# One addition on VectorE split by column: epsilon on the softmax sums of two heads

## The chip, the core and the metric

The kernel runs on one core of a Trainium2 chip. The metric is device time in microseconds (us) of one execution of the whole program. The names of the engines are those of the profile: PE is TensorE's matrix multiplication and PEld its weight load, DVE is VectorE, ACT is ScalarE, POOL is GpSimd, SP issues most transfers. Each engine works through its own instructions in the order in which they stand in the program, and waits where an instruction needs another engine's result.

## What is computed

Attention that keeps the 32 largest scores of each row, then a feed-forward layer, then a layer of 8 experts of which each token uses two.

```python
def _attn_ref(q, k, v):                       # batch 4, heads 8, sequence 576, head size 64
    scores = scale * np.matmul(q, k.transpose(0, 1, 3, 2))
    kth = np.partition(scores, -top_k, axis=-1)[..., -top_k:-top_k + 1]    # top_k = 32
    scores = np.where(scores >= kth, scores, -1000000000.0)
    scores = scores - np.max(scores, axis=-1, keepdims=True)
    attn = np.exp(scores)
    attn = attn / (np.sum(attn, axis=-1, keepdims=True) + 1e-09)
    return np.matmul(attn, v)
...
def _moe_ref(x, w_in, w_out):                 # 2304 tokens, 512 -> 2048 -> 512
    h = np.maximum(x @ w_in, 0.0)
    return h * h @ w_out
...
def _moe2_ref(x, ...):                        # the two best of 8 experts for each token
    out[mask] += top2_w[mask, k, None] * (np.maximum(x[mask] @ w1[e], 0.0) @ w2[e])
```

## The kernel before

Attention is cut into 80 units. A unit is 128 query rows of two heads (64 units, `pair_full`) or the 64 query rows left over, of two heads side by side on the partitions (16 units, `pair_left`). For each head of a unit PE makes 128 x 576 scores (L356), ACT copies them out of PSUM into `sb` (L359), and DVE searches the 32nd largest value: six pieces of 96 columns with MAX8 and MATCH_REPLACE8 (L367, L368), then rounds on the candidates (L369, L372, L374). POOL makes the bounds (`keep`, L390), ACT and POOL build the mask (L394, L395), and ACT takes the exponential and, in the same instruction, its sum over the row into one column of `sm` (L396). So in a full unit `sm` has two columns, one for each head; in a left unit one column is used.

`recip` then adds epsilon to `sm` (L401) and takes the reciprocal (L402), both on DVE. POOL spreads it (`rb`, L428), PE transposes the weights and `rb` (L407, L430, L431) and multiplies by V (L444), and DVE scales the result into `x` (L416, or L420 for left units). ACT and POOL split `x` into two parts for the matmuls of the next layer (L421, L422).

Units overlap: unit i + 2 is started while unit i is finished. Between these steps the program issues pieces of the feed-forward layer of tokens that are done (`step`; PE L272 to L288, ACT L292 to L295, POOL L296), of the routing, and, for the first 32 of 80 units, the conversion of the feed-forward weights (DVE L149 and L150, POOL L152 and L156). All of attention lies in the first 811 us. After it stand what is left of the feed-forward layer and the experts (PE L518 to L573).

A scheduler places the instructions: it keeps a priority for each (the order of the program, moved by an offset; `recip` and `finish` are moved ahead by 300, the feed-forward pieces back by 350) and a simulated time line, and so one instruction more can shift the order of others.

Of the kernel before, what the change touches and what calls it, by code (L numbers as in the profile page):

```python
# [14 lines left out]
ALU = mybir.AluOpType  # L15
# [4 lines left out]
EPS = 1e-9  # L20
# [32 lines left out]
def attention_ffn_moe(ctx: ExitStack, tc: tile.TileContext, q, k, v, w_ffn, w_route, noise, w_exp, out,  # L53
# [3 lines left out]
    nc = tc.nc  # L57
# [46 lines left out]
    for t, (b, i) in enumerate(tiles):  # L104
        if i == 0:
            nc.gpsimd.iota(tok_i[:, t:t + NFULL], pattern=[[P, NFULL]], base=b * S, channel_multiplier=1)
        elif i is None:
            nc.gpsimd.iota(tok_i[:, t:t + 1], pattern=[[0, 1]], base=b * S + NFULL * P, channel_multiplier=1)
            nc.gpsimd.tensor_scalar(tok_i[LEFT:P, t:t + 1], tok_i[LEFT:P, t:t + 1], 1.0, float(S - LEFT),
                                    op0=ALU.mult, op1=ALU.add)  # L110
# [287 lines left out]

    def recip(sm):
        with tc.high_priority(SOON):  # L400
            nc.vector.tensor_scalar(sm, sm, 1.0, EPS, op0=ALU.mult, op1=ALU.add)  # L401
            nc.vector.reciprocal(sm, sm)  # L402

    def transpose4(e):
# [43 lines left out]
    def pair_full(b, j, qt):  # L448

        hA = 2 * j  # L450
        q0 = 2 * (j % 2)
        es = []
        sm = apool.tile([P, 2], F32, name="sm", bufs=6)
        lf = apool.tile([P, 2, D], F32, name="lf", bufs=4)
        for i in range(2):
            kt = K4[b, j // 2][:, (hA + i) % 4]
            t = scores([(qt[:, 0, q0 + i, :], kt), (qt[:, 1, q0 + i, :], kt)])
            softmax(*t, sm[:, i:i + 1])
            left_keys(lf, i, t[0])
            es.append(t[0])  # L460
            yield
        recip(sm)
        pts = [transpose4(es[0])]
        yield
        pts.append(transpose4(es[1]))
        yield
        t5 = rest(es, sm, lf)
        yield
        yield times_v(b, hA, pts, t5)

    def pair_left(b, j, qt):
        hA = 2 * j
        q0 = 2 * (j % 2)
        st = []
        for i in range(2):
            kt = K4[b, j // 2][:, (hA + i) % 4]
            st += [(qt[:, 0, q0 + i, :], kt), (qt[:, 1, q0 + i, :], kt)]
        sm = apool.tile([P, 2], F32, name="sm", bufs=6)
        lf = apool.tile([P, 2, D], F32, name="lf", bufs=4)
        t = scores(st)  # L480
        e = t[0]
        softmax(*t, sm[:, 0:1])
        for i in range(2):
            left_keys(lf, i, e)
        yield
        yield
        recip(sm[:, 0:1])
        pt = transpose4(e)
        yield
        yield  # L490
        t5 = rest([e, e], sm[:, 0:1].to_broadcast([P, 2]), lf)
        yield
        yield times_v(b, hA, [pt, pt], t5)
# [302 lines left out]
    for e in range(E):  # L796
        nc.vector.tensor_scalar(over[:, e:e + 1], base[:, e:e + 1], float(-(e * NT + CAP)), 0.0,
                                op0=ALU.add, op1=ALU.max)
# [180 lines left out]
```

## Time and profile before

| | before |
|---|---|
| median of 3 runs | 1419.05 us (1416.67 to 1421.17) |
| the profiled execution | 1419.02 us |
| its span, first to last instruction | 1417.2 us |
| PE busy | 1261.8 us (89%) |
| DVE busy | 970.6 us (68%) |
| ACT busy | 844.6 us (60%) |
| POOL busy | 798.2 us (56%) |

The profiled execution lies 1.8 us above its span, and at the median. The shares are means over two very different stages: attention, up to about 811 us, and what follows. Matmuls overlap one another in the records, so a PE that is busy all the time is not thereby at its peak.

### The profile page before, as it was taken

The numbers are of one execution on the slowest core, as the hardware profiler recorded it, in microseconds if no ns is written. First come the engines' busy times: TensorE is split into PE (matmuls) and PEld (weight loads), VectorE is DVE, ScalarE is ACT, GpSimd is POOL, SyncE is SP. The second block draws the span as 40 slices with busy tenths as digits, with TensorE's granted clock in tenths as the row PEclk, the third lists the DMA queues.
The fourth block names the chain that finished last, engine by engine and source line by source line (L and its number), as shares of the span: only waits on it lengthen the run. The fifth ranks groups of instructions, "written<-read, shape, count | busy, mean of one in ns | idle before, by whom it ended". The sixth has DMA issues, their size and how long they took to land. (4 is left out here: it accounts for less than half of the span.)

```text
span 1417.2 us, 26382 instructions
## 1 busy us (share of the span) xinstructions
PE 1261.8 (89%) x7937; PEld 1085.0 (77%) x7937; DVE 970.6 (68%) x5025; ACT 844.6 (60%) x1741; POOL 798.2 (56%) x1366
## 2 busy tenths in 40 slices
PE   2576559899899899999999999999989999999996
PEld 1354347787788788787887888789778999989995
DVE  8999989999988899999999100145563434444342
ACT  5768768888886887897887534344443233333321
POOL 4869889896787776877756532605233315133131
PEclk9877769999999999999999999999999999999998
DMA  9984558961557345535533586836564435344241
GB/s 328 346 306 151 188 170 295 314 236 61 167 192 259 105 139 180 189 127 175 178 105 120 193 276 214 284 112 231 185 215 141 146 112 163 116 146 135 89 144 37
DMA packets 85241, 257.50 MB, mean 182 GB/s; under 512 B 10716, under 2 KB 10844, under 8 KB 85088
## 3 DMA queue, kind: packets, MB, share of 16 engines
q1 hardware_dynamic: 75808, 227.32, 48.5%
q0 software_dynamic: 9280, 28.40, 5.5%
q8 instruction: 65, 1.06, 0.3%
q14 instruction: 88, 0.72, 0.2%
HBM read 205.71 MB, written 52.06 MB: 182 GB/s over the span
## 5 line engine op out<-in xcount | busy, mean ns | idle before, releaser
L395 POOL TENSOR_TENSOR sb<-sb,w 128x576 f32<-128x576 f32 x144 | 207.6, 1448 | 17.8 <-ACT w L394 14.5
L368 DVE MATCH_REPLACE8 w<-m,sb 128x96 f32<-128x96 f32 x864 | 200.8, 242 | 0.0
L578 DVE SCALAR_TENSOR_TENSOR ht<-ph,ht 128x384 fp32r<-128x384 f32 (+1 forms) x128 | 62.7, 490 | 182.1 <-ACT ht L577 181.9
L577 ACT ACTIVATE ht<-ph 128x384 fp32r<-128x384 f32 (+1 forms) x128 | 55.9, 437 | 216.5 <-PE ph L573 216.5
L593 POOL DMA_INDIRECT out<-y,info x40 | 44.9, 1122 | 244.6 <-DVE y L592 238.0
L367 DVE MAX8 m<-sb 128x8 f32<-128x96 f32 x864 | 165.1, 244 | 19.3 <-ACT sb L359 16.1
L356 PE MATMUL ps<-K,qt 128*128 128x288 f32 x640 | 133.6, 335 | 40.1 <-POOL K L324 15.9
L571 PE MATMUL ph<-xe,wi 128*128 128x384 f32 (+1 forms) x512 | 159.6, 312 | 2.5 <-DVE xe L523 2.2
L572 PE MATMUL ph<-xe,wi 128*128 128x384 f32 (+1 forms) x512 | 159.5, 312 | 0.8 <-DVE xe L523 0.8
L573 PE MATMUL ph<-xe,wi 128*128 128x384 f32 (+1 forms) x512 | 159.2, 311 | 0.2 <-DVE wi L565 0.2
L356 PEld LDWEIGHTS ps<-K,qt 128*128 128x128 f32 x640 | 104.5, 210 | 52.6 <-ACT sb L359 20.1
L296 POOL TENSOR_TENSOR gt<-r,gt 128x384 fp32r<-128x384 f32 x96 | 97.8, 1019 | 63.6 <-ACT gt L295 57.7
L407 PE MATMUL pa<-ident,sb 128*128 128x128 f32 x576 | 99.4, 297 | 36.2 <-DVE x L416 13.0
L552 PE MATMUL acc<-wo,ht 128*128 128x512 f32 x320 | 126.5, 398 | 0.9 <-DVE y L592 0.8
L286 PE MATMUL pf<-xT,wi 128*128 128x384 f32 x320 | 115.4, 361 | 13.3 <-ACT r L292 5.8
L394 ACT ACTIVATE w<-sb,keep 128x576 f32<-128x576 f32 x144 | 110.2, 776 | 26.3 <-POOL keep L390 25.9
L553 PE MATMUL acc<-wo,ht 128*128 128x512 f32 x320 | 125.4, 394 | 0.0
L396 ACT ACTIVATE sb<-sb,keep 128x576 f32<-128x576 f32 x144 | 112.2, 780 | 21.2 <-POOL sb L395 20.9
L287 PE MATMUL pf<-xT,wi 128*128 128x384 f32 x320 | 111.9, 350 | 4.8 <-POOL xT L422 4.8
L272 PE MATMUL acc<-wo,gt 128*128 128x512 f32 x288 | 112.8, 403 | 3.0 <-DMA wo<-wsc 1.5
L407 PEld LDWEIGHTS pa<-ident,sb 128*128 128x128 f32 x576 | 68.2, 149 | 60.8 <-issue 22.8
L273 PE MATMUL acc<-wo,gt 128*128 128x512 f32 x288 | 111.0, 396 | 0.0
(181 smaller groups left out, 3547.8 us busy)
## 6 DMA issues: line engine op xcount, KB each, us to landing
wi<-wsc SPq DMA_DIRECT2D x96, 512.0 KB, 4.5
wo<-wsc SPq DMA_DIRECT2D x96, 512.0 KB, 4.5
raww<-in_exp SPq DMA_DIRECT2D x80, 512.0 KB, 3.6
raw<-in_ffn SPq DMA_DIRECT2D x32, 512.0 KB, 4.3
wsc<-csp SPq DMA_DIRECT2D x32, 512.0 KB, 3.9
xs<-xr SPq DMA_DIRECT2D x40, 258.0 KB, 7.4
mr<-xs SPq DMA_DIRECT2D x40, 258.0 KB, 3.4
qn<-in_q SPq DMA_DIRECT2D x40, 256.0 KB, 3.7
```

The source lines that it names most:

```text
L272: nc.tensor.matmul(acc[tt], gt[:, 0, sl], wo[:, 0, :], start=(f == 0), stop=False)
L286: nc.tensor.matmul(ph[:, 0:n], wi[:, 0, sl], xT[:, 0, c, 0:n], start=(c == 0), stop=False)
L356: nc.tensor.matmul(ps[:, n, 0:HS], st, kt[:, n * HS:(n + 1) * HS], start=(i == 0), stop=(i == len(pairs) - 1))
L367: nc.vector.max(top, sb[:, sl])
L368: nc.vector.match_replace(out=w[:, sl], in_to_replace=top, in_values=sb[:, sl], imm_value=NEG)
L395: nc.gpsimd.tensor_tensor(sb, sb, w, op=ALU.subtract)
L407: nc.tensor.transpose(pt[:, c * P:(c + 1) * P], e[:, c * P:(c + 1) * P], ident)
L552: nc.tensor.matmul(acc[t], hs[i][:, 0, sl], wo[:, 0, :], start=(f == 0), stop=False)
L553: nc.tensor.matmul(acc[t], hs[i][:, 0, sl], wo[:, 1, :], start=False, stop=False)
L571: nc.tensor.matmul(ph[:, 0:n], wi[:, 0, sl], xe[i][:, 0, c, :], start=(c == 0), stop=False)
L572: nc.tensor.matmul(ph[:, 0:n], wi[:, 0, sl], xe[i][:, 1, c, :], start=False, stop=False)
L573: nc.tensor.matmul(ph[:, 0:n], wi[:, 1, sl], xe[i][:, 0, c, :], start=False, stop=(c == NC - 1))
```

## The change

The addition of epsilon is issued once for each column of `sm`, where it was one instruction on all columns. The 64 full units have two columns, so they issue two additions in place of one. The 16 left units hand over one column and keep their one instruction. The reciprocal stays one instruction on all columns. Since a line is added, what stood at L402 and below is one line lower after the change (the additions at L402, the reciprocal at L403, and so on).

```diff
     def recip(sm):
         with tc.high_priority(SOON):
-            nc.vector.tensor_scalar(sm, sm, 1.0, EPS, op0=ALU.mult, op1=ALU.add)
+            for i in range(sm.shape[1]):
+                nc.vector.tensor_scalar(sm[:, i:i + 1], sm[:, i:i + 1], 1.0, EPS, op0=ALU.mult, op1=ALU.add)
             nc.vector.reciprocal(sm, sm)
```

DVE's rows of the second unit's start, while the first unit's two heads wait for their sums. Before the change, the search of one head stands there without an addition:

```order
L372 MAX m<-cand 128x8
L367 MAX m<-sb 128x8 x6
L368 MATCH_REPLACE w<-m,sb 128x96 x6
L367 MAX m<-sb 128x8
L369 MAX m<-w 128x8
L367 MAX m<-sb 128x8 x5
L372 MAX m<-m 128x8
```

After the change:

```order
L372 MAX m<-cand 128x8
L367 MAX m<-sb 128x8 x6
L368 MATCH_REPLACE w<-m,sb 128x96 x6
L402 TENSOR_SCALAR sm<-sm 128x1
L367 MAX m<-sb 128x8
L369 MAX m<-w 128x8
L367 MAX m<-sb 128x8 x5
L372 MAX m<-m 128x8
```

The addition for the unit's first head now stands here by itself, ahead of the pieces of the next head.

Some rows further on DVE, one search later, stands the addition that was there before, and the reciprocal. Before the change:

```order
L367 MAX m<-sb 128x8 x6
L368 MATCH_REPLACE w<-m,sb 128x96 x6
L401 TENSOR_SCALAR sm<-sm 128x2
L367 MAX m<-sb 128x8
L369 MAX m<-w 128x8
L402 RECIPROCAL sm<-sm 128x2
L368 MATCH_REPLACE w<-m,sb 128x96 x6
```

After the change:

```order
L367 MAX m<-sb 128x8 x6
L368 MATCH_REPLACE w<-m,sb 128x96 x6
L402 TENSOR_SCALAR sm<-sm 128x1
L367 MAX m<-sb 128x8
L369 MAX m<-w 128x8
L403 RECIPROCAL sm<-sm 128x2
L368 MATCH_REPLACE w<-m,sb 128x96 x6
```

The second head's addition keeps the place of the old one, on one column, and the reciprocal stays where it was. From the third unit on, the finer order of all engines differs at many places; DVE has 64 rows of attention more, no other engine has more or fewer.

## Rows read from the trace of the kernel before

**Rows 1.** Busy us (instructions) of each engine by stretch; granted clock, DMA share, GB/s.

```profile
core 0: us, PE busy (x) PEld busy (x) DVE busy (x) ACT busy (x) POOL busy (x), PEclk, DMA share, GB/s
50.00:100.00 50.00, 28.68 (x191) 21.89 (x192) 48.78 (x301) 33.98 (x67) 33.52 (x47) 0.73 0.98 350
100.00:200.00 100.00, 57.40 (x352) 43.17 (x353) 95.80 (x534) 76.45 (x153) 88.13 (x108) 0.69 0.49 168
200.00:300.00 100.00, 88.50 (x564) 75.89 (x561) 95.14 (x530) 82.86 (x172) 92.36 (x107) 0.94 0.82 278
300.00:400.00 100.00, 93.22 (x696) 77.30 (x696) 98.84 (x663) 85.44 (x186) 75.36 (x137) 1.00 0.43 139
400.00:500.00 100.00, 95.23 (x679) 80.88 (x677) 86.22 (x571) 74.27 (x161) 74.02 (x116) 0.97 0.54 184
500.00:600.00 100.00, 97.14 (x692) 83.55 (x692) 93.14 (x608) 83.30 (x178) 75.54 (x130) 1.00 0.51 173
600.00:700.00 100.00, 95.05 (x685) 82.48 (x684) 98.03 (x658) 82.38 (x179) 72.80 (x131) 0.98 0.49 158
700.00:780.00 80.00, 77.14 (x572) 63.68 (x571) 76.18 (x504) 63.01 (x138) 50.02 (x104) 1.00 0.36 120
780.00:813.00 33.00, 33.00 (x238) 28.32 (x238) 5.71 (x18) 17.30 (x40) 17.59 (x27) 1.00 0.56 186
...
1100.00:1300.00 200.00, 200.00 (x1138) 181.04 (x1137) 87.11 (x145) 62.79 (x125) 59.79 (x125) 1.00 0.43 135
```

**Rows 2.** PE in order of time near 305 us: start, us, instruction.

```profile
305.07 0.34 PE L287 MATMUL pf<-xT,wi 128*128 128x384 f32 x1
305.25 0.34 PE L288 MATMUL pf<-xT,wi 128*128 128x384 f32 x1
```

**Rows 3.** DVE groups by shape, whole span: busy us, mean ns, idle before.

```profile
L401 DVE TENSOR_SCALAR sm<-sm 128x2 f32<-128x2 f32 x64 | 36.8, 575 | 4.1 <-ACT sb L396 3.9
...
L401 DVE TENSOR_SCALAR sm<-sm 128x1 f32<-128x1 f32 x16 | 2.2, 139 | 1.3 <-ACT sb L396 1.3
```

**Rows 4.** Line L401 alone: duration ns min/median/max, first and last start.

```profile
L401 DVE TENSOR_SCALAR sm<-sm x80: 127/167/3485, 42.7 to 788.9; 128x2 f32<-128x2 f32 x64, 128x1 f32<-128x1 f32 x16
```

**Rows 5.** All engines in order of time, 300.2 to 301.4 us.

```profile
300.31 1.00 POOL L296 TENSOR_TENSOR gt<-r,gt 128x384 fp32r<-128x384 f32 x1
300.38 0.21 DVE L372 MAX8 m<-cand 128x8 f32<-128x56 f32 x1
...
300.50 0.84 DVE L401 TENSOR_SCALAR sm<-sm 128x2 f32<-128x2 f32 x1
...
301.25 0.28 DVE L416 TENSOR_TENSOR x<-pa,t 128x128 f32<-128x128 f32 x1
```

**Rows 6.** All engines in order of time, 113.4 to 113.8 us.

```profile
113.48 1.28 POOL L324 TENSOR_TENSOR qt<-qn,qt 128x512 fp32r<-128x512 f32 x1
113.54 0.14 DVE L401 TENSOR_SCALAR sm<-sm 128x1 f32<-128x1 f32 x1
...
113.59 0.08 DVE L368 MATCH_VALUE_LOAD w<-m,sb 128x8 f32 x1
```

**Rows 7.** DVE groups by shape, 0 to 300 us.

```profile
L401 DVE TENSOR_SCALAR sm<-sm 128x2 f32<-128x2 f32 x20 | 15.4, 771 | 0.0
...
L401 DVE TENSOR_SCALAR sm<-sm 128x1 f32<-128x1 f32 x4 | 0.5, 134 | 0.0
```

**Rows 8.** DVE's waits, 40 to 800 us: total us, times, longest.

```profile
DVE m L367 <- ACT sb L359: 15.7, 12, 3.6
DVE x L416 <- PE pa L444: 12.3, 5, 5.7
DVE sm L401 <- ACT sb L396: 5.2, 5, 1.4
```

**Rows 9.** PE's waits, 40 to 800 us.

```profile
PE pa L407 <- DVE x L416: 13.0, 7, 3.9
```

**Rows 10.** DVE in order of time at the end of attention.

```profile
780.24 1.57 DVE L785 TENSOR_TENSOR late<-keep 128x144 f32<-128x144 f32 x1 [0.42 <-POOL keep L390]
...
811.00 0.29 DVE L416 TENSOR_TENSOR x<-pa,t 128x128 f32<-128x128 f32 x1 [4.84 <-PE pa L444]
```

## The prediction

> **What bounds the kernel now.** I first read the busy time by stretch, because the shares on the page are means over two stages. Up to 780 us DVE is the fullest engine in most stretches: 48.78 of 50 us, then 95.80, 95.14 and 98.84 of 100 [rows 1]. PE, the engine with the largest total, is at 57.40 of 100 us between 100 and 200 us. Its 93 to 97 later on look like a full engine and are not: two matmuls of the feed-forward layer start 0.18 us apart where nothing holds them, and each is booked for 0.34 us [rows 2]. So PE has room during attention, and it waits for DVE there, for example 13.0 us at L407 for DVE's `x` [rows 9]. POOL comes near its end only between 200 and 300 us, with 92.36 of 100 [rows 1].
>
> After the last search the picture turns. DVE compares the kept bounds of all searches at 780.24 us, and its last `x` is at 811.00 us, after a wait for PE [rows 10]; PE is busy for all 33.00 us of that stretch, and for 200.00 of 200 us among the experts [rows 1]. So the time is, roughly, what DVE needs for its searches up to 780 us, plus a fixed piece of PE work behind it. Time that DVE saves before 780 us can shorten the whole; after it DVE's time is worth nothing, and the change touches nothing there, since the last addition starts at 788.9 us [rows 4].
>
> **What the changed instruction costs today.** The groups by shape hold the main finding. The addition on two columns takes 575 ns in the mean, 64 times, 36.8 us; on one column the same operation takes 139 ns, 16 times [rows 3]. One more column can't cost 436 ns of arithmetic. The line's durations run from 127 ns over a median of 167 to 3485 [rows 4], so most instances are short and a part of them is held for a long time while it is booked as busy. The order in time shows by what: at 300.50 us a two-column addition starts while POOL is in a TENSOR_TENSOR from 300.31 to 301.31, and it ends at 301.34, just behind POOL's end [rows 5]. A one-column addition at 113.54 us falls inside a POOL instruction of 1.28 us and still takes 0.14 us [rows 6]. None of the 16 can have been held long: with a minimum of 127 ns [rows 4] and a mean of 139 [rows 3], the longest is at most 16 x 139 - 15 x 127 = 319 ns.
>
> The Trainium skill has a rule for this: "SBUF — State Buffer", section "Who interferes with whom", says that VectorE in a mode that uses two ports and GpSimd exclude each other from a shared port pair for a whole instruction, and that tensor_scalar is an operation that can enter such a mode. The rows of the two-column form agree.
>
> **The sum.** Each full unit trades one two-column addition for two one-column ones.
> - Removed: 64 x 575 ns = 36.8 us. Added: 128 x 139 ns = 17.8 us. By durations DVE gains 19.0 us [rows 3].
> - DVE instructions overlap at their edges: the next one starts at 301.25, 0.09 us before the addition's end at 301.34 [rows 5], and at 113.59, 0.09 us before 113.68 [rows 6]. Each of the 64 additional instructions hides as much, 5.8 us in all, so by starts the gain is up to 24.8 us. I take the middle, 22 us, and keep 19.0 and 24.8 as bounds.
> - Where it falls: up to 300 us 20 of the 64 take 15.4 us; 40 short ones would take 40 x 0.139 = 5.6 [rows 7, 3], a gain of 9.8 of 19.0, or 52%. Of the 22 us, 11.4 lie before 300 us and 10.6 after.
> - What of it passes on: between 50 and 300 us DVE is busy for 239.7 of 250 us, but POOL is at 92.36 in the last 100 of them [rows 1] and would stop some of it; I let 80% pass, 9.1 us. From 300 to 780 us DVE is busy for 452.4 of 480 us, so it idles for 27.6 us [rows 1], mostly for scores from ACT and products from PE [rows 8]. Where DVE gets ahead of those it only waits longer; I let 60% pass, 6.4 us. Both shares are choices, the first nearer to all since almost no idle time stands there.
> - What is added besides: the first head's addition now stands alone in DVE's queue, ahead of the pieces of the next search, and waits for its own exponential. Behind it stand those searches, and behind them ACT, PE and POOL of the next heads. Today 5 of the 80 additions wait, for 5.2 us in all [rows 8]; 64 more at that rate would wait 4.2 us. A third of it falls on time that counts, the rest where DVE would have waited for scores anyway: 1.5 us. The bounds are nothing and the full 4.2.
> - The reciprocal, the DMAs and the instructions of PE, ACT and POOL stay the same in number. The scheduler's order moves them finely. Counted in the two orders, 1545 of the 2016 matmuls of the feed-forward layer stand ahead of attention's last product with V before the change and 1557 after it, so nearly the same work is left behind; I cost this at nothing. If PE had no room for those 12 during attention, they would be worth 12 x 0.18 = 2.2 us [rows 2] the other way.
>
> 9.1 + 6.4 - 1.5 = 14.0 us, against the profiled execution's 1419.02 us, which is the median's 1419.05 within 0.1: **1405.0 us**. The least by the bounds is 19.0 x 0.4 - 4.2 = 3.4 us gained (1415.6), the most all of 24.8 (1394).
>
> **The rivals.** 0.3%, or 4.3 us, is about what a measurement can tell from no change.
> - The gain is absorbed. DVE gets ahead and waits instead, for scores from ACT or products from PE, since ACT and PE are at 82 to 97 of 100 us after 200 us [rows 1], and for POOL between 200 and 300 us. With a quarter of 22 us passed on less 1.5, the time is 1415; with none, 1419 to 1420. For it speaks that a POOL that is held up less or more hides such shifts; against it that DVE idles for only 27.6 of 480 us [rows 1].
> - Slower: the first head's addition stops DVE's queue. It sits one search earlier than the joint one and needs the exponential of its head, which comes last in a chain of ACT and POOL. A wait today is 5.2 / 5 = 1.04 us [rows 8]. From a mean of 22 / 64 = 0.34 us for each of the 64 the gain is eaten; if every second waited for 1.04 us, DVE would lose 33 us against 22, and at 0.7 passed on the time would be 1419 + 8 = 1427. Against it: 75 of 80 additions wait for nothing today.
> - The change doesn't do what it says: the one-column form is held as well. Then 128 x 0.575 = 73.6 us stand in place of 36.8, and at 0.7 passed on the time would be 1419 + 26 = 1445. The 16 one-column rows speak against it [rows 3, 6]. The Trainium skill, "VectorE: DVE Perf Modes", section "What auto-detection actually checks", lets the two-port mode begin where the outermost dimensions other than one are even or equal in source and destination, and a single column in place is equal to itself; taken so, the page would give this rival, and the trace is against that reading.
> - The order is luckier than counted, or short additions also free POOL: more than 24.8 us, under 1394.
>
> **How the numbers follow.** A part of the gain passes on, 1394 to 1415: 0.78, likeliest 1405. Absorbed, 1415 to 1421: 0.11. Addition stops the queue, 1427: 0.04. One column held too, 1445: 0.03. Under 1394: 0.04. The range is 1394 to 1417: it takes in the bounds of the sum and about half of the absorbed case, and leaves out 0.055 + 0.04 + 0.03 + 0.04 = 0.165. Faster by over 0.3% is under 1414.8: 0.82. Within: 0.11. Slower: 0.07.
>
> **What would show it.** In the profile after, the group of one-column additions should count 144 with a mean near 140 ns and none far above 320, about 20 us in all. The joint group of 64 should be gone. DVE's comparison of the kept bounds should come some 12 to 16 us before 780, and the last `x` as much before 811, with the same PE time behind. If DVE's idle time for ACT's scores and PE's products grows by about 20 us and that comparison stays where it is, the gain was absorbed. If DVE waits for ACT's L396 grow to tens of us, the early addition stops the queue. If one-column additions of 1 us and more appear, the form doesn't matter. The prediction is wrong, too, if other DVE instructions that run beside POOL take up the time that the additions gave back.

## The result, and the profile after

The changed kernel takes 1400.56 us (median of 4 runs, 1397.0 to 1402.39) against 1418.57 us of the kernel before beside it (1416.67 to 1421.17): a ratio of 0.9865, 95% interval 0.9843 to 0.9887, so 1.1 to 1.6% faster. The forecast was 1405.0 in a range of 1394 to 1417. The profiled execution took 1400.43 us with a span of 1398.7 us, 18.5 us less than before.

DVE's groups by shape in the kernel after (busy us, mean ns, idle before), which answer to [rows 3]:

```profile
L150 DVE SCALAR_TENSOR_TENSOR ca<-raw,ca 128x512 uint32<-128x512 uint32 x32 | 35.0, 1094 | 0.1
L149 DVE TENSOR_SCALAR ca<-ca 128x512 uint32<-128x512 uint32 x32 | 29.1, 910 | 2.2 <-ACT ca L148 2.1
L402 DVE TENSOR_SCALAR sm<-sm 128x1 f32<-128x1 f32 x144 | 20.2, 140 | 5.4 <-ACT sb L396 5.1
```

The same view of the kernel before, for the two lines that were not shown:

```profile
L150 DVE SCALAR_TENSOR_TENSOR ca<-raw,ca 128x512 uint32<-128x512 uint32 x32 | 34.3, 1072 | 0.1
L149 DVE TENSOR_SCALAR ca<-ca 128x512 uint32<-128x512 uint32 x32 | 23.2, 724 | 0.6 <-ACT ca L148 0.6
```

There are 144 additions at 140 ns, 20.2 us in place of the 36.8 + 2.2 us of [rows 3]. One thing has grown: the shift in the weights' conversion, L149, also a TENSOR_SCALAR and unchanged in the program, takes 29.1 us in place of 23.2. The additions' line by itself after (duration ns min/median/max), beside [rows 4]:

```profile
L402 DVE TENSOR_SCALAR sm<-sm x144: 125/140/167, 36.6 to 772.3; 128x1 f32<-128x1 f32 x144
```

The longest of 144 is 167 ns, where it was 3485. In the trace 84 of the 144 begin and end inside one POOL instruction, so this is not for want of occasions. In the kernel before, the trace ties the long ones to POOL one by one: 37 of the 64 two-column additions took over 200 ns, each of them began while POOL was in an instruction, and each ended 0.02 to 0.08 us behind the end of a POOL instruction; of the 18 that began with POOL idle, none took over 170 ns. An instruction that waits in this way, booked as busy, is called held below.

Busy time by stretch after, columns as in [rows 1]:

```profile
50.00:100.00 50.00, 32.10 (x213) 24.67 (x212) 48.77 (x312) 34.92 (x72) 34.31 (x48) 0.76 0.97 346
100.00:200.00 100.00, 61.02 (x360) 45.85 (x359) 96.09 (x564) 79.64 (x156) 90.43 (x111) 0.64 0.49 168
200.00:300.00 100.00, 87.31 (x564) 73.05 (x564) 95.75 (x538) 83.91 (x178) 92.67 (x111) 0.95 0.81 275
...
700.00:780.00 80.00, 76.44 (x587) 65.25 (x584) 65.02 (x439) 61.67 (x137) 48.59 (x101) 1.00 0.35 120
780.00:813.00 33.00, 31.88 (x200) 27.71 (x199) 1.64 (x9) 12.17 (x26) 16.57 (x23) 1.00 0.80 286
...
1100.00:1300.00 200.00, 200.00 (x1143) 180.81 (x1142) 87.39 (x146) 65.09 (x129) 69.52 (x157) 1.00 0.44 140
```

DVE is as full as before, but gets through more: 564 instructions in place of 534 between 100 and 200 us, 7 of the 30 more being additions. It is still the fullest engine there, with POOL now at 90.43 us. The end of attention comes earlier. DVE in order of time there, beside [rows 10]:

```profile
765.70 0.39 DVE L786 TENSOR_TENSOR late<-keep 128x144 f32<-128x144 f32 x1 [1.56 <-POOL keep L390]
...
795.46 0.29 DVE L417 TENSOR_TENSOR x<-pa,t 128x128 f32<-128x128 f32 x1 [7.09 <-PE pa L445]
```

The comparison behind the last search starts at 765.70 us in place of 780.24, 14.5 us earlier, and the last `x` at 795.46 in place of 811.00, 15.5 us earlier. DVE's waits of 40 to 800 us, beside [rows 8]:

```profile
DVE x L417 <- PE pa L445: 19.1, 6, 7.1
DVE m L367 <- ACT sb L359: 13.5, 10, 3.0
...
DVE sm L402 <- ACT sb L396: 5.1, 7, 1.6
```

The wait for PE seems to have grown from 12.3 to 19.1 us, but a window that ends at 800 us cuts off the last waits of the kernel before, whose attention ends at 811; over the whole span it went from 25.9 us down to 19.1. Nearly all of it, 23.3 us before and 18.4 after, lies behind the last search, where it costs nothing. The waits for scores are no longer than they were, and the additions wait for 5.1 us in all, as before, though they are 144.

**The account.** To see where DVE's time went I summed, from both traces, for each kind of DVE instruction up to that comparison, the time from its start to the start of the next one or to its own end, whichever is first, so that nothing is counted twice.

| up to the end of the searches, us | before | after | change |
|---|---|---|---|
| additions (78 and 143 of them) | 32.6 | 10.5 | -22.1 |
| conversion, L149 and L150 | 52.8 | 59.3 | +6.5 |
| all other DVE work | 650.7 | 650.9 | +0.2 |
| DVE idle | 42.8 | 43.7 | +0.9 |
| sum | | | -14.5 |

Behind it, on PE: the last product of attention is a further 1.0 us earlier (it starts at 795.1 us, where it was 810.6); the feed-forward layer then ends 112.8 us later in place of 114.9, with 459 of its matmuls left in place of 471, 2.1 us; and the experts' part is the same, 484.9 us against 484.8 from their first matmul to the last. The writes at the end took 0.9 us less. 14.5 + 1.0 + 2.1 + 0.9 = 18.5.

### The profile page after: what moved, and what is told of

Same layout as the page of the kernel before. It is cut to its first block, busy times and chain, and to the rows that moved or that the text cites. A ratio compares the mean times of both kernels' runs of the same rounds, so it can differ in the third digit from the quotient of the medians.

```text
span 1398.7 us, 26415 instructions
## 1 busy us (share of the span) xinstructions
PE 1256.0 (90%) x7937; PEld 1084.3 (78%) x7937; DVE 954.0 (68%) x5089; ACT 842.5 (60%) x1741; POOL 798.0 (57%) x1366
## 4 chain that ended last, share of the span: by engine, by line
PE 50%; DVE 31%; DMA 6%; ACT 5%; POOL 4%; issue 3%; SPq 0%; POOLq 0%; DVEq 0%; ACTq 0%
DVE w L368 9%; DVE m L367 6%; PE ph L573 5%; PE ph L572 5%; PE ph L574 5%; PE acc L555 5%; PE acc L553 5%; PE acc L554 5%; DVE m L369 4%; DVE cand L374 4%; DVE m L372 3%; PE acc L274 2%; PE acc L272 2%; PE acc L273 2%; PE pa L445 2%
## 5 line engine op out<-in xcount | busy, mean ns | idle before, releaser
L367 DVE MAX8 m<-sb 128x8 f32<-128x96 f32 x864 | 168.2, 244 | 16.4 <-ACT sb L359 14.8
L286 PE MATMUL pf<-xT,wi 128*128 128x384 f32 x320 | 112.1, 350 | 6.8 <-ACT r L292 4.0
L287 PE MATMUL pf<-xT,wi 128*128 128x384 f32 x320 | 109.3, 341 | 4.8 <-POOL xT L423 4.8
```

The costliest lines, as they stand in the source:

```text
L367: nc.vector.max(top, sb[:, sl])
```

## The experiments

In the two series below the kernel before took 1428.67 and 1428.28 us, about 10 us more than at first, so ratios to it are compared and not times. Theory A: an addition on several columns waits while POOL works, one on a single column doesn't. Theory B: the gain comes from issuing a unit's additions apart, the first one earlier, or from the order that the scheduler happens to make. The edits are shown against the changed kernel.

**Two additions a unit, but two columns wide.**

```diff
-            for i in range(sm.shape[1]):
-                nc.vector.tensor_scalar(sm[:, i:i + 1], sm[:, i:i + 1], 1.0, EPS, op0=ALU.mult, op1=ALU.add)
-            nc.vector.reciprocal(sm, sm)
+            n = sm.shape[1]
+            wide = apool.tile([P, 2, 2], F32, name="wide", bufs=6)
+            for i in range(n):
+                nc.vector.tensor_scalar(wide[:, i, :], sm[:, i:i + 1].to_broadcast([P, 2]), 1.0, EPS,
+                                        op0=ALU.mult, op1=ALU.add)
+            nc.vector.reciprocal(sm, wide[:, 0:n, 0])
```

> One addition for each head as after the change, in the same places of the program, but each writes two columns (the head's sum read twice, into a tile of its own, of which the reciprocal takes one column); the left units' additions too are two columns wide. Theory A, that the two-column form waits for POOL: 144 additions at the 575 ns of before, 83 us in place of 20 us after the change; DVE has 46 us more than in the kernel before, and at 0.7 passed on the time is about 1450 us (1430 to 1465). Theory B, that the gain comes from issuing the heads' additions apart, or from the order that the scheduler makes of it: as after the change, 1400 us, with additions at 140 to 170 ns.

1444.82 us, 1.0128 of before (1.0089 to 1.0167), so slower. DVE's groups by shape of this kernel:

```profile
L404 DVE TENSOR_SCALAR wide<-sm 128x2 f32<-128x2 f32 x144 | 71.2, 495 | 6.7 <-ACT sb L396 6.6
```

As many instructions at the same places of the program as in the changed kernel, one more column each (the sum read twice, into a tile of its own), and 71.2 us in place of 20.2. This is what tells the theories apart: issuing the additions apart is not the gain, and without the short form it costs 1.3%. The 495 ns are near the 575 expected. Again the long ones go with POOL: 73 of the 144 took over 200 ns, out of the 103 that began while POOL was in an instruction, and of the other 41 none took over 169.

The scheduler's order is no rival here. DVE's first 1084 instructions stand in the same order in this kernel and in the changed one, and so do those of PE, ACT and POOL up to there. The last of the 1084, in the changed kernel and then in this one:

```profile
196.47 0.23 DVE L368 MATCH_REPLACE8 w<-m,sb 128x96 f32<-128x96 f32 x1
205.99 0.24 DVE L368 MATCH_REPLACE8 w<-m,sb 128x96 f32<-128x96 f32 x1
```

By the way of counting of the account above, the 29 additions up to there take 1.7 us in the changed kernel and 14.4 here; the conversion takes 35.2 us there and 32.7 here. So 12.7 us less of additions brought DVE there 9.5 us sooner, and 2.5 us of the difference went into the conversion.

**One joint instruction of a kind that doesn't wait.**

```diff
-            for i in range(sm.shape[1]):
-                nc.vector.tensor_scalar(sm[:, i:i + 1], sm[:, i:i + 1], 1.0, EPS, op0=ALU.mult, op1=ALU.add)
+            nc.vector.reduce_sum(out=sm, in_=sm.unsqueeze(2), axis=mybir.AxisListType.X)
             nc.vector.reciprocal(sm, sm)
```

> One instruction on both columns as before the change, but a sum over one element in place of the addition (epsilon is left out), an operation that the Trainium skill, SBUF - State Buffer, section Who interferes with whom, says never contends with GpSimd on this chip. Theory A, the wait for POOL: about 150 to 180 ns each without long ones, some 13 us in place of 39, 64 instructions fewer than after the change: 1392 to 1402 us. Theory B, the additions apart or the order: as before, 1415 to 1421 us.

1408.39 us, 0.9861 of before (0.9833 to 0.9890). The same view:

```profile
L401 DVE TENSOR_REDUCE sm<-sm 128x2 f32<-128x2 f32 x64 | 9.1, 142 | 1.6 <-ACT sb L396 1.5
...
L401 DVE TENSOR_REDUCE sm<-sm 128x1 f32<-128x1 f32 x16 | 2.2, 140 | 2.1 <-ACT sb L396 2.1
```

One instruction for both columns, as before the change, and at the old place, gives the whole gain, because it takes 142 ns in place of 575. PE's instructions stand in the order of the kernel before up to 463 us, and there PE is 9.4 us ahead of it. The rule of the Trainium skill that the expectation names ("SBUF — State Buffer", section "Who interferes with whom") fits: none of the 80 took more than 155 ns.

**No addition.**

```diff
-            for i in range(sm.shape[1]):
-                nc.vector.tensor_scalar(sm[:, i:i + 1], sm[:, i:i + 1], 1.0, EPS, op0=ALU.mult, op1=ALU.add)
             nc.vector.reciprocal(sm, sm)
```

> No addition at all (epsilon is left out), the reciprocal alone. Theory A: the waits for POOL are gone and the 20 us of one-column additions too; DVE starts its next instruction 0.05 to 0.06 us after a short addition starts, so 144 of them are worth 7 to 9 us of DVE time and, at 0.7, 5 to 6 us: 1393 to 1397 us. Theory B, that the gain needs the two additions apart: 1415 us or more. If the fixed price of an added instruction is nothing: 1400.

1412.71 us, 0.9893 (0.9865 to 0.9920). Faster than before, which speaks against the additions apart as the source of the gain, but not below the changed kernel as A had it. The same view shows one thing that the kernel after doesn't have:

```profile
L150 DVE SCALAR_TENSOR_TENSOR ca<-raw,ca 128x512 uint32<-128x512 uint32 x32 | 39.9, 1246 | 0.1
L149 DVE TENSOR_SCALAR ca<-ca 128x512 uint32<-128x512 uint32 x32 | 26.8, 836 | 1.9 <-ACT ca L148 1.9
L401 DVE RECIPROCAL sm<-sm 128x2 f32<-128x2 f32 x64 | 9.8, 154 | 6.3 <-ACT sb L396 6.3
```

The conversion's L150 takes 39.9 us, 4.9 more than after the change, and the reciprocals wait for the exponentials. So a part of the time that was taken out came back in other DVE instructions. The account above, against the kernel with the joint reduction, says how much: up to the end of the searches the conversion takes 61.8 us in place of 54.3 and all other DVE work 654.9 in place of 649.6, which is more than the 5.6 us of reductions and 2.9 us of idle time that are gone.

**Each one-column addition twice.**

```diff
             for i in range(sm.shape[1]):
-                nc.vector.tensor_scalar(sm[:, i:i + 1], sm[:, i:i + 1], 1.0, EPS, op0=ALU.mult, op1=ALU.add)
+                for _ in range(2):
+                    nc.vector.tensor_scalar(sm[:, i:i + 1], sm[:, i:i + 1], 1.0, EPS, op0=ALU.mult, op1=ALU.add)
```

> Each one-column addition issued twice: 288 in place of 144. Theory A: none is held, all near 140 ns, 40 us in place of 20; by starts 7 to 9 us more of DVE time, the second waiting for the first perhaps 0.1 us more each (14 us): 1405 to 1415 us. If the one-column form were held as often as the two-column one and had only been lucky, a good part of 288 would take over 200 ns and the time would pass 1430 us.

1419.15 us, 0.9937 (0.9917 to 0.9957). The line alone, 288 additions:

```profile
L403 DVE TENSOR_SCALAR sm<-sm x288: 94/141/156, 36.1 to 788.3; 128x1 f32<-128x1 f32 x144
```

None over 156 ns. The one-column form is not held in 288 more instances, and 144 more of them, 20 us by durations, cost 0.9937 - 0.9861 = 0.76%, about 11 us, if the ratio is set against that of the changed kernel in the second series.

**The second series.** The changed kernel once more, unedited:

> The changed kernel once more, beside the next three. Ratio to before 0.984 to 0.989 as at first; additions 144 at 140 ns.

1408.55 us, 0.9861 (0.9840 to 0.9883), as at first. With it, three columns in place of two (in the first edit above, `[P, 2, 3]` and `to_broadcast([P, 3])`):

> As e1_pairs, but three columns in place of two, an odd number, equal in source and destination. Theory A1, that the wait comes with any width over one column: 144 additions of which 4 in 10 are over 200 ns, about 70 us in all, and 1.01 to 1.015 of before, as e1_pairs. Theory A2, that an odd width is free of it: 144 additions near 140 ns, 20 us, and the time of the changed kernel, 0.985.

1448.11 us, 1.0135 (1.0094 to 1.0175, from two runs). The groups by shape:

```profile
L404 DVE TENSOR_SCALAR wide<-sm 128x3 f32<-128x3 f32 x144 | 69.9, 486 | 7.0 <-ACT sb L396 6.8
```

An odd width waits like an even one: 73 of the 144 took over 200 ns, as with two columns, all of them begun while POOL was in an instruction. It is the single column that is free.

Then the order alone. The next two, the kernel without additions and the changed kernel, deal out the feed-forward pieces a little otherwise:

```diff
-FILLS = [0.02, 0.1, 0.15, 0.2, 0.15, 0.1, 0.2, 0.1]
+FILLS = [0.02, 0.12, 0.15, 0.2, 0.15, 0.1, 0.18, 0.1]
```

> e3_no_add with the feed-forward pieces dealt out a little otherwise within a unit (0.12 and 0.18 of a unit's share in place of 0.10 and 0.20 at two places): the same instructions, another fine order. e3_no_add had less DVE work than e2_joint_reduce and was not faster (0.9893 against 0.9861). If that is the luck of the order, a new order moves it by several us either way, 0.984 to 0.993. If taking instructions out has a cost of its own, 0.988 to 0.990 again.

1413.58 us, 0.9898 (0.9875 to 0.9921): where it was. L150 took 41.3 us there, again more than the 35.2 us of the changed kernel beside it. But this does not test whether the missing gain was the luck of one order: in the traces all engines keep the order of the kernel without additions up to 521 us, and the conversion is over by then.

> The changed kernel with the same other order as e6_no_add_shift. The additions stay at 144 near 140 ns. If the gain is the wait that is gone, it stays within the spread that the order makes, 0.982 to 0.992; if the gain was the luck of one order, it can go to 0.995 or more.

1415.96 us, 0.9909 (0.9888 to 0.9930). Its additions and conversions take what they do in the changed kernel; what differs most is how long DVE idled. The groups by shape:

```profile
L149 DVE TENSOR_SCALAR ca<-ca 128x512 uint32<-128x512 uint32 x32 | 27.5, 860 | 2.5 <-ACT ca L148 2.4
L402 DVE TENSOR_SCALAR sm<-sm 128x1 f32<-128x1 f32 x144 | 20.3, 141 | 11.5 <-ACT sb L396 11.2
```

Here the additions wait for 11.5 us in place of 4.8 in the changed kernel beside it (7.0 in place of 2.8 up to the comparison behind the searches), and DVE idles for 52.9 us between 50 us and that comparison in place of 44.4. This order, which differs from 438 us on, costs half a per cent, a third of what the change gave. The kernel before was not run with these pieces, so what they would do to it is not known; that the order doesn't make the gain rests on the first two experiments.

## Why the prediction was right

**The bound and the mechanism.** DVE sets the time up to the last search and PE behind it, as the prediction had it: the searches end 14.5 us earlier, the last `x` 15.5, within the 12 to 16 that it named. The gain is the wait of two-column additions for POOL. It goes with the form (71 us with two columns, 70 with three, 20 with one, in equal numbers and places, and up to 196 us in the same order of all engines), and a joint instruction that doesn't wait brings it all.

**The price of the additions.** 22 us were taken between the bounds of 19.0 and 24.8; 22.1 were measured by the account above.

**What passes on.** 9.1 + 6.4 = 15.5 us, less 1.5 for the first head's addition, were to arrive; 14.5 arrived at the end of the searches. The sum was close, the reason given for the loss was not. DVE was to get ahead and wait longer for scores and products; its idle time grew by 0.9 us. The loss is in the conversion instead, 6.5 us, which the prediction named as its last way of going wrong but did not price. That the sum came out close is partly luck. The conversion lies before 300 us, so of the 11.8 us that the additions gave back up to the fiftieth search about half was kept, where 80% were forecast; of the 10.3 us behind it nearly all was kept, where 60% were forecast. Nor must the time go into the conversion: set against the same profile of the kernel before, the joint reduction gave back 27.1 us, the conversion took only 1.5 us more, DVE idled 12.3 us more, as the forecast had it, and the searches ended 14.3 us earlier. The 1.5 us for the addition that stands alone did not come: 5.1 us of waits for 144 additions against 5.2 for 80. (In the other order above they waited for 11.5.)

**What was left out of the sum.** The 12 feed-forward matmuls that the scheduler moved ahead of the end of attention were costed at nothing. PE had room for them, and they brought 2.1 us (by the prediction's price, 12 x 0.18 us, it would be 2.2); with 1.0 us on the way from the last search to the last product and 0.9 us in the last writes that makes the 4 us between 14.5 and 18.5, and so most of the 4.5 us between the forecast's 14.0 and the 18.5 by which the spans differ.

**The rivals.** That the one-column form is held too is refuted by 144 + 288 of them with a longest of 167 ns; so the trace is against reading the condition "equal" of the Trainium skill's page "VectorE: DVE Perf Modes", section "What auto-detection actually checks", as met by a single column. Three columns, equal in source and destination, meet it, and they do wait (73 of 144 over 200 ns). The absorbed gain and the addition that stops the queue did not come, though each is seen in part: the first in the conversion, the second in the other order. More than 24.8 us did not come either. One reading of the rows was off, without weight in the sum: ACT is not at 82 of 100 us or more all the way after 200 us, but at 74.27 between 400 and 500 [rows 1].

**What stays open.** Why the kernel without any addition keeps less of the gain (0.9893 and 0.9898, the intervals overlapping those of the changed kernel) is not settled: its conversions and other DVE work are longer, but what makes them so was not tried, and the other order left that stretch as it was. A version of the conversion that doesn't wait for POOL wasn't tried either. None of the kernels beat the changed one clearly.

## What to carry to other kernels

When an instruction of almost no work has a mean far above its median, look at what the other engines do during its longest instances before asking what it costs to have more of them: here 64 more instructions took 22 us off DVE. On VectorE a TENSOR_SCALAR on two or three columns beside a busy GpSimd waited here for up to 3.5 us, and two one-column instructions (280 ns), or a reduction on both columns (142 ns), were shorter than one of 575 ns. Count what the freed time runs into next: in the changed kernel three tenths of it went into the weights' conversion on the same engine.

## What was not expected of the hardware

A held instruction is not always let in when POOL's current instruction ends. Of the 37 held additions of the kernel before, 29 ended just behind the first end of a POOL instruction, in 25 cases although POOL went straight on to its next; the other 8 lasted past one to five ends more, at each of which POOL went straight on. What decides between the two was not found. DVE's longest addition there, in order of time:

```profile
445.30 3.48 DVE L401 TENSOR_SCALAR sm<-sm 128x2 f32<-128x2 f32 x1
```

and POOL meanwhile:

```profile
444.37 2.79 POOL L395 TENSOR_TENSOR sb<-sb,w 128x576 f32<-128x576 f32 x2
447.14 0.65 POOL L437 TENSOR_SCALAR lf<-sb 128x64 f32<-128x64 f32 x3
447.75 1.00 POOL L296 TENSOR_TENSOR gt<-r,gt 128x384 fp32r<-128x384 f32 x1
448.73 0.23 POOL L437 TENSOR_SCALAR lf<-sb 128x64 f32<-128x64 f32 x1
```

The addition lasts until 448.78 us, past the ends of two TENSOR_TENSOR, three small ones and a third TENSOR_TENSOR, each of which starts 0.02 to 0.04 us before the one ahead of it ends. The same happened after the change to L149 on DVE:

```profile
223.58 4.48 DVE L149 TENSOR_SCALAR ca<-ca 128x512 uint32<-128x512 uint32 x1
```

It ended at 228.06 us, and POOL went from one instruction to the next without a gap until 227.77 us. With 3.9 us over the 0.58 us of that line's median this one instance is most of the growth of L149, 5.9 us. It returns with the same order, at 3.37 us in the second run of the changed kernel, and not with the joint reduction, where no L149 took more than 2.12 us. The reciprocal, which works on the same two columns, is never held: 9.6 us for 64, as before, with a longest of 174 ns, though 31 of the 64 begin and end inside one POOL instruction.
